# A recurrent-memory attention step on one core: output-projection weights cut by 4 heads x 512 outputs, and the chunks of two steps interleaved

## Chip, cores and metric

One core of a Trainium2 chip runs one program, one launch. The metric is device time in microseconds (us); the kernel before has a median of 2463.49 us in three runs (2462.24 to 2467.92).

## What is computed

```python
# x 2048 x 1024; 32 heads of 128; memory of M = 8 rows; segments of 32 rows; F = 3584
mem = mem0
for s in range(64):
    h = concat([mem, x[32*s : 32*s+32]])            # 40 rows
    q, k, v = h @ Wq, h @ Wk, h @ Wv                # 1024 -> 32 heads x 128
    p = softmax(mask(q @ k.T * 128**-0.5))          # per head, 40 x 40
    o = (p @ v) @ Wo                                # 4096 -> 1024
    mem = o[:8]; a[32*s : 32*s+32] = o[8:]
b = (gelu(x @ w_gate) * (x @ w_up)) @ w_down
g = sigmoid((x * gate_w).sum(-1))
out = g * a + (1 - g) * b
```

The 64 segments are serial: the first 8 rows of one segment's output are the memory rows of the next. The feed-forward part (`b`) is not.

## The kernel before, in words

A prologue turns and stores x, then 64 **steps** (one per segment) run, then the output projection of rows that were left out of the steps, then the feed-forward part with the final mix.

**Rows.** A step works on 32 columns: 24 rows of x and the 8 memory rows, in `hT` (8 chunks of 128 x 32). The other 8 rows of x of each segment need no memory; their k, q and v are computed for four segments at once by **fills** (`fill`, L689), and stored to DRAM (`qk_scr`, `v_scr`) to be read back by the steps (`load_qk`, `load_v`). The table `FILL` gives the steps two, two, one and one fill in turn, of eight matmul groups each; the two kinds of step are called two-fill and one-fill below. No fill is made in the last steps.

**Pieces.** The four weight matrices take 64 **pieces** of 128 x 2048 bf16 (512 KB); memory holds 50. So each matrix is cut in two halves of 16 heads (`u` = 0, 1) and eight pieces each (`i`), and some pieces of the two halves share a slot (`PAIRS`: 3 of k, 3 of q, 4 of v, 4 of o). A step does one half in round `r` = 0 and the other in `r` = 1; in the next step the halves change places. A shared slot's piece is used in `r` = 1 and again in the next step's `r` = 0, and then, through `spent`, SP fetches the other half's piece into the slot (`fetch`, L351), due in `r` = 1 of the same step. Per step that is 14 fetches of 512 KB. `seq` puts shared pieces first in `r` = 0 and last in `r` = 1.

**Order.** `ORDER` lists the groups of a step: k0 q0 v0 k1 q1 o0 v1 o1 (matrix and round), eight pieces each (L662 for k, q, v; L674 for o). All engines run their instructions in program order, with waits that a small planner (`_Prog`) derives from the memory regions that each operation reads and writes. Between pieces the lists `at` put the rest: ACT evacuates a finished group into `tok` (L561), PE transposes it (L578), DVE copies it to `kT` or `qT` (L564), GpSimd adds the rest columns (`put_rest`, L723); `scores` (L597, L602) then starts a chain on DVE and ACT (L606 to L622) that ends in `tA` and `tB`, and `attend` (L632, L637) multiplies by v and leaves `oT`. There are two such chains in a step, one per round.

**End of a step.** `o1` finishes one bank, ACT copies it to `a_bf`, PE transposes it (L837), DVE puts the 8 memory rows into `hT` (L840), and the next step's k0 begins. A part of the last fill's matmuls lies around these transposes; its result goes out of `oS` to DRAM in the next step (`pend`, `fill_evac`, `fill_put`, L700 and L719). `oS` and `vA` (v of round 0) are the same memory.

Of the kernel before, what the change touches and what calls it, by code (L numbers as in the profile page):

```python
# [195 lines left out]
def bass_gated_mix__memory_aug_recurrent_mem_tr__geglu_ffn__prompt_kernel(  # L196
# [34 lines left out]
    with ExitStack() as es:  # L231
# [16 lines left out]
        a_scr = nc.dram_tensor("a_scr", [NSEG, SEG, D], BF16)  # L248
# [21 lines left out]
        hT = al("hT", [128, KC, 32])  # L270
        hR = al("hR", [128, KC, 32])
        low = cur[0] = (cur[0] + 63) // 64 * 64
        qkr = al("qkr", [128, 2, 128])
        oRc = al("oRc", [128, NB, 32])
        vB = al("vB", [128, 2, 128])
        kT = al("kT", [128, 4, 4, LQ])
        qT = al("qT", [128, 4, 4, LQ])
        oT = al("oT", [128, 4, 4, LQ])
        tok = al("tok", [128, 512])
        vA = al("vA", [128, 4, 128], at=oT.off)  # L280
        pA = al("pA", [128, 8, 32], at=kT.off)
        pB = al("pB", [128, 288], at=kT.off + 512)
        E8 = al("E8", [128, 8, LQ], at=qT.off + 640)
        tA = al("tA", [128, 8, 32], at=qT.off)
        tB = al("tB", [128, 8, 32], at=qT.off + 512)
        a_bf = al("a_bf", [128, 256], at=qT.off)
# [8 lines left out]
        PAIRS = {"k": (1, 3, 5), "q": (0, 2, 5), "v": (0, 2, 4, 6), "o": (0, 2, 4, 6)}  # L295
# [5 lines left out]
        ORDER = (("k", 0), ("q", 0), ("v", 0), ("k", 1), ("q", 1), ("o", 0), ("v", 1), ("o", 1))  # L301
        walk = [(m, r, i) for m, r in ORDER for i in seq(m, r)]

        def at_step(p, s):
            m, r, i = walk[p]
            return (m, r ^ (s % 2), i)
# [13 lines left out]
        for s_ in range(NSEG):  # L320
            for p in range(64):
                k = at_step(p, s_)
                uses[home[k]].append(k)
# [6 lines left out]
        def src(k):  # L330
            m, u, i = k
            if m == "o":
                h0 = 16 * u + 2 * i
                return A_Wo[h0:h0 + 2].rearrange("h p f -> p h f")
            W = {"q": A_Wq, "k": A_Wk, "v": A_Wv}[m]
            return W[i * 128:(i + 1) * 128, 16 * u:16 * u + 16, :].rearrange("d h e -> d (h e)")

        def dst(t, k):
            return t[:, :].rearrange("p (h f) -> p h f", h=2) if k[0] == "o" else t[:, :]
# [4 lines left out]
        def fetch(n):  # L344
            k, t = uses[n][done[n]], slots[n]
            if paired(k):
                lane = f"sl{n}"
            else:
                lane = f"res{nlane[0] % 8}"
                nlane[0] += 1  # L350
            op("sp", lambda e: e.dma_start(dst(t, k), src(k)), wr=[t.r()], lane=lane)  # L351
# [80 lines left out]
        def load_h(s, eng="sp"):  # L432
            op(eng, lambda e: e.dma_start(hT[:, :, :].rearrange("p k c -> p (k c)"), xq_scr[s // 4, :, s % 4, :]),
               rd=[("D", "xq", s // 4)], wr=[hT.r()], lane=f"h{eng}")
# [5 lines left out]
        def load_qk(s, r, eng="pool"):  # L440
            u = r ^ (s % 2)
            op(eng, lambda e: e.dma_start(qkr[:, :, :], qk_scr[:, s, 2 * u:2 * u + 2, :]),
               rd=[("D", "qk", s // 4, 2 * u), ("D", "qk", s // 4, 2 * u + 1)], wr=[qkr.r()], lane=f"qkr{eng}")
# [11 lines left out]
        load_x(2)  # L455
        for n, p in enumerate(range(16)):
            first(at_step(p, 0))
            if n + 3 < NPX:
                load_x(n + 3)
        op("pe", tr_mem, rd=[pm.r(), ident.r()], wr=[BK(5)])  # L460
        op("dve", lambda e: e.tensor_copy(memT[:, :], PBV[5][:, 0:64]), rd=[BK(5)], wr=[memT.r()])
        for T in range(NT):
            do_x(T)
            load_x(T + NPX)
            if T == 0:
                load_h(0, "pool")
                op("dve", lambda e: e.tensor_copy(hT[:, :, NR:32], memT[:, :].rearrange("p (k c) -> p k c", k=KC)),
                   rd=[memT.r()], wr=[hT.r()])
        for p in range(16, 24):
            first(at_step(p, 0))  # L470
# [65 lines left out]
        def load_a(T):  # L536
            t = asb[T % 4]
            op("act", lambda e: e.dma_start(t[:, :], a_scr[4 * T:4 * T + 4].rearrange("s t f -> (s t) f")),
               rd=[("D", "a", s) for s in range(4 * T, 4 * T + 4)] + [("D", "ar", T // 4, h) for h in range(2)], wr=[t.r()],
               lane=f"al{T % 4}")  # L540
# [6 lines left out]
        rbs = [al(f"rb{i}", [128, D], at=kT.off + 2048 * i) for i in range(2)]  # L547
# [5 lines left out]
        def load_xo():  # L553
            for k in lost:
                op("sp", lambda e, k=k: e.dma_start(dst(xo[k], k), src(k)), wr=[xo[k].r()], lane=f"xo{k[2]}")
# [19 lines left out]
        def trans(to, how):  # L575
            def f(e):
                for j in range(4):
                    ins = e.transpose(PBV[TT][:, j * 128:(j + 1) * 128], tok[:, j * 128:(j + 1) * 128], ident[:, :])  # L578
                return ins
            op("pe", f, rd=[tok.r(), ident.r()], wr=[BK(TT)])  # L580
            i_ap = PBV[TT][:, 0:512].rearrange("p (j g c) -> p (j g) c", g=4, c=32)
            o_ap = to[:, :, :, 0:32].rearrange("p j g c -> p (j g) c")
            n = 4 * LQ
            if how == "both":
                act_copy(o_ap[:, 0:8], i_ap[:, 0:8], [BK(TT)], [to.r(0, 2 * n)])
                dve_copy(o_ap[:, 8:16], i_ap[:, 8:16], [BK(TT)], [to.r(2 * n, 4 * n)])
            else:
                cp[how](o_ap, i_ap, [BK(TT)], [to.r()])
# [5 lines left out]
        def scores():  # L594

            def f(e):
                e.matmul(PB[SS][:, 0:320].rearrange("p (a c) -> p a c", a=4), lhsT=ident[:, :],  # L597
                         rhs=mS[:, :].unsqueeze(1).to_broadcast([128, 4, 80]), start=True, stop=False, skip_group_check=True)
                for lo, hi, c in ((0, 32, 0), (32, 40, 40)):
                    for j in range(4):  # L600
                        for g in range(4):
                            ins = e.matmul(PB[SS][32 * g:32 * g + hi - lo, j * 80 + c:j * 80 + c + LQ], lhsT=qT[:, j, g, lo:hi],  # L602
                                           rhs=kT[:, j, g, :], start=False, stop=True, skip_group_check=True)
                return ins
            op("pe", f, rd=[qT.r(), kT.r(), ident.r(), mS.r()], wr=[BK(SS)])
            op("pool", lambda e: e.memset(pB[:, :].bitcast(FP32), 0.0), wr=[pB.r()])  # L606
# [6 lines left out]
            op("dve", lambda e: e.tensor_tensor(out=pA[:, :, :], in0=E8[:, :, 0:32], in1=b8(sm, 32), op=ALU.mult),  # L613
               rd=[E8.r(), st8.r(8, 16)], wr=[pA.r()])
            fin = op("dve", lambda e: e.tensor_tensor(
                out=pB[:, :].rearrange("p (j a) -> p j a", j=4)[:, :, 0:64].rearrange("p j (c k) -> p j c k", c=2)[:, :, :, 0:8],
                in0=E8[:, :, 32:40].rearrange("p (j c) k -> p j c k", c=2),
                in1=sm.rearrange("p (j c) -> p j c", c=2).unsqueeze(3).to_broadcast([128, 4, 2, 8]), op=ALU.mult),
               rd=[E8.r(), st8.r(8, 16)], wr=[pB.r()])
            op("dve", lambda e: e.transpose(tA[:, :, :].rearrange("p a c -> p (a c)"), pA[:, :, :].rearrange("p a c -> p (a c)")),  # L620
               rd=[pA.r()], wr=[tA.r()])
            op("dve", lambda e: e.transpose(tB[:, :, :].rearrange("p a c -> p (a c)"), pB[:, 0:256]),  # L622
               rd=[pB.r()], wr=[tB.r()], after=[fin])

        def attend(u):
            bo = (B0, B1, B2, SS)

            def f(e):
                for j in range(4):
                    for g in range(4):  # L630
                        r = slice(32 * g, 32 * g + 32)
                        e.matmul(PB[bo[g]][:, j * LQ:(j + 1) * LQ], lhsT=vA[r, j, :],  # L632
                                 rhs=tA[r, 2 * j:2 * j + 2, :].rearrange("p a c -> p (a c)")[:, 0:LQ],
                                 start=(j == 0), stop=False, skip_group_check=True)
                for g in range(4):
                    r = slice(32 * g, 32 * g + 32)
                    ins = e.matmul(PB[bo[g]][:, 0:4 * LQ].rearrange("p (j c) -> p j c", j=4)[:, :, 24:40], lhsT=vB[r, u, :],  # L637
                                   rhs=tB[r, :, :].rearrange("p (j a) c -> p j (a c)", a=2)[:, :, 24:40],
                                   start=False, stop=True, skip_group_check=True)
                return ins  # L640
            op("pe", f, rd=[vA.r(), tA.r(), tB.r(), vB.r()], wr=[BK(b) for b in bo])
# [7 lines left out]

        KQV = [x for x in ORDER if x[0] != "o"]  # L650
        bank_of = {}

        def proj(p, s):
            k = at_step(p, s)
            w = slots[home[k]]
            i = k[2]
            if k[0] != "o":
                h, bk = hT, bank_of[walk[p][:2]]

                def f(e):  # L660
                    for g in range(4):
                        ins = e.matmul(PB[bk][32 * g:32 * g + 32, :], lhsT=h[:, i, :], rhs=w[:, g * 512:(g + 1) * 512],  # L662
                                       start=(p % 8 == 0), stop=(p % 8 == 7))
                    return ins
                op("pe", f, rd=[h.r(), w.r()], wr=[BK(bk)])
            else:
                r = walk[p][1]
                gp_, jj = i // 2, i % 2

                def f(e):  # L670
                    for hh in range(2):
                        for g in range(4):
                            c = hh * 1024 + g * 256
                            ins = e.matmul(PB[XO][32 * g:32 * g + 32, 0:256], lhsT=oT[:, gp_, 2 * jj + hh, 0:32],  # L674
                                           rhs=w[:, c:c + 256], start=(r == 0 and p % 8 == 0 and hh == 0), stop=(r == 1 and p % 8 == 7 and hh == 1))
                    return ins
                n = 4 * LQ
                op("pe", f, rd=[oT.r(gp_ * n, (gp_ + 1) * n), w.r()], wr=[BK(XO)])
            spent(k)

# [14 lines left out]
        def fill_evac(m, u, G, b, st):  # L695
# [7 lines left out]
            else:  # L703
                act_copy(tok[:, :], PB[b][:, :], [BK(b)], [tok.r()])

        def fill_put(m, u, G, st):
# [3 lines left out]

            def f(e):
                for j in range(4):
                    ins = e.transpose(PBV[TT][:, j * 128:(j + 1) * 128], tok[:, j * 128:(j + 1) * 128], ident[:, :])
                return ins
            op("pe", f, rd=[tok.r(), ident.r()], wr=[BK(TT)])
            op("dve", lambda e: e.tensor_copy(st[:, :].rearrange("p (i x c) -> p x i c", i=4, x=16),
                                              PBV[TT][:, 0:512].rearrange("p (x i c) -> p x i c", x=16, i=4)), rd=[BK(TT)], wr=[st.r()])
            m4 = 2 * u + (0 if m == "q" else 1)
            op("pool", lambda e: e.dma_start(qk_scr[:, 4 * G:4 * G + 4, m4, :], st[:, :].rearrange("p (i y) -> p i y", i=4)),  # L719
               rd=[st.r()], wr=[("D", "qk", G, m4)], lane="fq")  # L720

        def put_rest(t, m):
            op("pool", lambda e: e.tensor_copy(t[:, :, :, 32:40].rearrange("p j g c -> p (j g) c"),  # L723
                                               qkr[:, m, :].rearrange("p (x c) -> p x c", c=8)),
               rd=[qkr.r()], wr=[t.r()])

        base_of = {mr: 8 * n_ for n_, mr in enumerate(ORDER)}
        pend = []
        FILL = ((("k", 1), ("q", 1)), (("q", 0), ("v", 0)), (("v", 1),), (("k", 0),))
        X, Y = A0, A1  # L730
        for s in range(NSEG):
            last = s == NSEG - 1
            at = {}
# [3 lines left out]
            bank_of.update({mr: (X, Y)[n % 2] for n, mr in enumerate(KQV)})  # L737
# [253 lines left out]
```

## Time and profile before

| | |
|---|---|
| median of three runs | 2463.49 us |
| profiled execution | 2468.72 us, of which the span of instructions is 2466.9 us |
| granted TensorE clock, mean | 0.975 |
| start of the first k0 that follows a memory update to that of the last (62 steps) | 139.5 to 1771.2 us, 26.3 us a step |
| in that stretch | PE busy 1379.0 of 1631.7 us, DMA share 0.85, 304 GB/s |
| from 1808 us on (feed-forward) | PE busy 636.3 of 658.0 us, DMA share 0.40 |
| PE busy over the span | 2100.7 us, 85% |

The profile gives one execution. PE is TensorE's matmuls, PEld its weight loads, SPq and POOLq the instructions by which SyncE and GpSimd issue DMAs. "L662" is a line of the kernel before. In a row of the timeline the columns are start, length, engine, line, operation, output and input, count, and in brackets the idle time of that engine before it with what ended it. In the windows view a row is a stretch of time with its length, the busy time of each engine, the granted TensorE clock, the share of the DMA engines and the GB/s.

### The profile page before, as it was taken

How to read it: one execution, taken by the hardware profiler on the slowest of the kernel's cores; microseconds unless marked ns; L12 is line 12 of the kernel's file. 1: busy time of each engine (PE TensorE's matmuls, PEld its weight loads, DVE VectorE, ACT ScalarE, POOL GpSimd, SP SyncE). 2: the span in 40 equal slices, each digit the busy share in tenths (PEclk: the TensorE clock that was granted, in tenths of full speed). 3: DMA queues.
4: the chain of work that ended last, by engine and by line, in shares of the span. 5: the costliest groups of instructions: out<-in, count | busy, mean ns of one | idle time of the engine just before them, and what ended most of it. 6: DMA issues, size and time to landing. Idle time of an engine off the chain costs nothing.

```text
span 2466.9 us, 76488 instructions
## 1 busy us (share of the span) xinstructions
PE 2100.7 (85%) x34796; PEld 1055.6 (43%) x34822; DVE 899.5 (36%) x2119; ACT 572.5 (23%) x1175; POOL 402.6 (16%) x822
## 2 busy tenths in 40 slices
PE   2588888888888888888888888888879999999998
PEld 1244444444444444444444444443454444444443
DVE  3233333333333333333333333333304436264462
ACT  1122222222222222222222222222203213032130
POOL 5222212212122122212222122221100000000000
PEclk9789999999999999999999999999989999999999
DMA  9878888888888888888888888988894260713506
GB/s 358 329 271 293 310 325 287 321 313 286 314 303 282 318 298 285 318 319 289 323 305 290 313 308 287 325 299 294 305 312 147 71 219 1 249 41 112 179 1 222
DMA packets 283524, 642.68 MB, mean 261 GB/s; under 512 B 26504, under 2 KB 80264, under 8 KB 283200
## 3 DMA queue, kind: packets, MB, share of 16 engines
q1 hardware_dynamic: 263008, 604.93, 68.3%
q0 software_dynamic: 9824, 17.97, 2.4%
q10 hardware_dynamic: 10368, 14.88, 1.7%
q8 instruction: 273, 4.47, 0.7%
q14 instruction: 51, 0.42, 0.0%
HBM read 606.29 MB, written 31.39 MB: 258 GB/s over the span
## 4 chain that ended last, share of the span: by engine, by line
PE 45%; DMA 41%; DVE 6%; issue 3%; ACT 3%; POOL 1%; SPq 0%; ACTq 0%; POOLq 0%
DMA sl<-in_A_Wq_dram 17%; DMA sl<-in_A_Wo_dram 15%; PE pb L908 13%; PE pb L662 8%; PE pb L674 7%; PE pb L945 7%; PE pb L689 4%; DMA qk_scr<-oS 3%; PE pb L867 2%; PE pb L578 2%; DMA v_scr<-oS 1%; DMA wd<-in_B_w_down_dram 1%; DMA xr_scr<-xr 1%; DMA sl<-in_A_Wk_dram 1%; ACT tok L561 1%
## 5 line engine op out<-in xcount | busy, mean ns | idle before, releaser
L662 PE MATMUL pb<-sl,hT 128*32 128x512 bf16 x12288 | 792.1, 385 | 77.2 <-DMA sl<-in_A_Wq_dram 32.7
L662 PEld LDWEIGHTS pb<-sl,hT 128*32 128x32 bf16 x12288 | 322.3, 97 | 393.5 <-DMA sl<-in_A_Wq_dram 47.8
L674 PE MATMUL pb<-sl,oT 128*32 128x256 bf16 x8192 | 297.1, 285 | 50.3 <-DMA sl<-in_A_Wo_dram 39.3
L561 ACT ACTIVATE tok<-pb 128x512 bf16<-128x512 f32 x320 | 191.3, 598 | 358.4 <-PE pb L662 304.5
L674 PEld LDWEIGHTS pb<-sl,oT 128*32 128x32 bf16 x8192 | 205.7, 100 | 126.3 <-DMA sl<-in_A_Wo_dram 61.0
L689 PE MATMUL pb<-sl,hR 128*32 128x512 bf16 x3072 | 227.4, 392 | 7.8 <-issue 4.0
L908 PE MATMUL pb<-xT,wg 128*128 128x512 bf16 x896 | 211.8, 379 | 8.4 <-DVE GT L924 8.4
L908 PE MATMUL pb<-xT,wu 128*128 128x512 bf16 x896 | 211.7, 379 | 0.0
L646 POOL COPY oRc<-oT 128x128 bf16<-128x128 bf16 x128 | 96.7, 756 | 623.6 <-DVE oT L564 623.6
L945 PE MATMUL pb<-wd,GT 128*128 128x512 bf16 x876 | 193.4, 379 | 5.7 <-DMA wd<-in_B_w_down_dram 4.6
L561 ACT ACTIVATE vA<-pb 128x512 bf16<-128x512 f32 x128 | 76.4, 597 | 285.5 <-DMA v_scr<-oS 104.2
L916 ACT ACTIVATE s<-pb 128x512 f32<-128x512 f32 x112 | 66.8, 596 | 319.9 <-PE pb L908 300.4
L564 DVE COPY qT<-pb 128x512 bf16<-128x512 bf16 x128 | 54.4, 425 | 235.2 <-PE pb L578 225.3
L908 PEld LDWEIGHTS pb<-xT,wg 128*128 128x128 bf16 x896 | 86.9, 98 | 116.4 <-DVE GT L924 12.8
L564 DVE COPY kT<-pb 128x512 bf16<-128x512 bf16 x128 | 54.4, 425 | 223.3 <-POOL kT L723 123.0
L945 PEld LDWEIGHTS pb<-wd,GT 128*128 128x128 bf16 x896 | 87.2, 98 | 111.9 <-DMA wd<-in_B_w_down_dram 8.3
L632 PE MATMUL pb<-tA,vA 32*128 32x40 bf16 x2048 | 36.0, 178 | 115.6 <-DVE tB L622 110.5
L908 PEld LDWEIGHTS pb<-xT,wu 128*128 128x128 bf16 x896 | 87.6, 98 | 105.7
L917 DVE SCALAR_TENSOR_TENSOR tp<-s,pb 128x512 f32<-128x512 f32 x112 | 77.0, 688 | 133.9 <-ACT s L916 133.8
L607 DVE TENSOR_REDUCE st<-pb 128x8 f32<-128x320 f32 x128 | 63.0, 492 | 164.3 <-PE pb L602 164.3
L609 ACT ACTIVATE E<-pb 128x320 bf16<-128x320 f32 x128 | 55.7, 435 | 241.9 <-DVE pb L608 241.8
L561 ACT ACTIVATE oT<-pb 128x160 bf16<-128x160 f32 x256 | 63.8, 301 | 193.2 <-PE pb L637 193.2
(77 smaller groups left out, 1761.8 us busy)
## 6 DMA issues: line engine op xcount, KB each, us to landing
sl<-in_A_Wv_dram SPq DMA_DIRECT2D x268, 512.0 KB, 11.0
sl<-in_A_Wo_dram SPq DMA_DIRECT2D x268, 512.0 KB, 7.2
sl<-in_A_Wk_dram SPq DMA_DIRECT2D x205, 512.0 KB, 5.7
sl<-in_A_Wq_dram SPq DMA_DIRECT2D x205, 512.0 KB, 8.9
wd<-in_B_w_down_dram SPq DMA_DIRECT2D x56, 1024.0 KB, 5.7
wg<-in_B_w_gate_dram SPq DMA_DIRECT2D x3, 1792.0 KB, 15.4
wu<-in_B_w_up_dram SPq DMA_DIRECT2D x3, 1792.0 KB, 14.2
qkr<-qk_scr POOLq DMA_DIRECT2D x65, 64.0 KB, 5.8
```

Of the source, the lines that this page charges most:

```text
L561: op("act", lambda e: e.activation(o, i, ACTF.Copy), rd=rd, wr=wr)
L564: op("dve", lambda e: e.tensor_copy(o, i), rd=rd, wr=wr)
L607: op("dve", lambda e: e.tensor_reduce(nm, sS, AX.X, ALU.max, negate=True), rd=[BK(SS)], wr=[st8.r(0, 8)])
L609: op("act", lambda e: e.activation(E8[:, :, :].rearrange("p a c -> p (a c)"), PB[SS][:, 0:320], ACTF.Exp, scale=scale), rd=[BK(SS)], wr=[E ...
L646: op("pool", lambda e: e.tensor_copy(oRc[:, :, 16 * u:16 * u + 16].rearrange("p c x -> p x c"), oT[:, :, :, 32:40].rearrange("p g j c -> p ...
L662: ins = e.matmul(PB[bk][32 * g:32 * g + 32, :], lhsT=h[:, i, :], rhs=w[:, g * 512:(g + 1) * 512], start=(p % 8 == 0), stop=(p % 8 == 7))
L674: ins = e.matmul(PB[XO][32 * g:32 * g + 32, 0:256], lhsT=oT[:, gp_, 2 * jj + hh, 0:32], rhs=w[:, c:c + 256], start=(r == 0 and p % 8 == 0 ...
L689: ins = e.matmul(PB[b][32 * g:32 * g + 32, :], lhsT=h[:, k[2], :], rhs=w[:, g * 512:(g + 1) * 512], start=(n == 0), stop=(n == 7))
L908: ins = e.matmul(PB[bk][:, 0:FB], lhsT=w[:, kc, cc:cc + 128], rhs=xT[:, :, :, kc, :].rearrange("p t i c -> p (t i) c"), start=(kc == 0), s ...
L916: op("act", lambda e, hg=hg: e.activation(s1[:, :], hg, ACTF.Square, scale=SQ), rd=[BK(bg)], wr=[s1.r()])
L917: op("dve", lambda e, hg=hg, t=t: e.scalar_tensor_tensor(out=t[:, :], in0=s1[:, :], scalar=1.0, in1=hg, op0=ALU.add, op1=ALU.mult), rd=[BK ...
L945: ins = e.matmul(PB[bank[2 * k + hf]][:, :], lhsT=GT[:, j, tb * 128:(tb + 1) * 128], rhs=w[:, jj, hf * 512:(hf + 1) * 512], start=(j == 0) ...
```

## The change

Wo's pieces hold 4 heads x 512 outputs where they held 2 heads x 1024. With that, the first four pieces of a half (`i` = 0..3) give outputs 0..511 and the last four outputs 512..1023. The shared slots become 2 of k, 2 of q, 6 of v and 4 of o (pieces 4..7); the sum stays 14. The groups of eight are cut in halves of four and are walked in the order `HEAD` + `BODY`: a step begins with the first half of k0, then does the second half of the **previous** step's o1, and then the first halves of q0 and v0, which need only chunks 0..3 of `hT`, before the second halves. So the memory rows come in two lots: `fold(s, 0)` and `next_mem(s, 0)` ahead of k0, `fold(s, 1)` and `next_mem(s, 1)` behind the o1 half. `hT` exists twice. A piece of Wo gives two partial sums on different partitions, which `fold` adds on DVE (two instructions of 64 x 256); ACT's copy to `a_bf` goes.

To make room, `tok` is gone: each evacuation goes to the memory of its target (`stage["k"]` is `kT`, `stage["q"]` is `qT`), `tA` and `tB` become one tile with one DVE transpose (`tAB`, in `qT`'s memory), the q columns of the rest are read from `qkr` directly, and GpSimd copies only k's. The last fill of a step now goes out through `qS`, not `oS`. All fills but the first of a two-fill step stand at the step's end. The shared Wo pieces are copied once to a DRAM scratch in steps 1 to 8 (`keep`) and from then on fetched from there in rows of 4 KB.

```diff
-        hT = al("hT", [128, KC, 32])
+        hT0 = al("hT0", [128, KC, 32])
+        vB = al("vB", [128, 2, 128])
+        hT1 = al("hT1", [128, KC, 32])
+        hT = (hT0, hT1)
+        part = tuple(al(f"part{n}", [128, 256], FP32, at=o) for n, o in enumerate((hT0.off, vB.off)))
...
-        tok = al("tok", [128, 512])
+        pAB = al("pAB", [128, 544], at=kT.off)
+        E8 = al("E8", [128, 8, LQ], at=qT.off + 384)
+        tAB = al("tAB", [128, 512], at=qT.off)
...
-        PAIRS = {"k": (1, 3, 5), "q": (0, 2, 5), "v": (0, 2, 4, 6), "o": (0, 2, 4, 6)}
+        PAIRS = {"k": (0, 1), "q": (0, 1), "v": (0, 1, 2, 3, 4, 5), "o": (4, 5, 6, 7)}
...
-        ORDER = (("k", 0), ("q", 0), ("v", 0), ("k", 1), ("q", 1), ("o", 0), ("v", 1), ("o", 1))
+        HEAD = [("k", 0, 0), ("o", 1, 1), ("q", 0, 0), ("v", 0, 0), ("k", 0, 1), ("q", 0, 1), ("v", 0, 1)]
+        BODY = [(m, r, h) for m, r in (("k", 1), ("q", 1), ("o", 0), ("v", 1)) for h in range(2)] + [("o", 1, 0)]
...
-                h0 = 16 * u + 2 * i
-                return A_Wo[h0:h0 + 2].rearrange("h p f -> p h f")
+                h0 = 16 * u + 4 * (i % 4)
+                return A_Wo[h0:h0 + 4, :, 512 * (i // 4):512 * (i // 4) + 512].rearrange("h p f -> p h f")
...
+        def load_piece(t, k, lane):
+            if k in kept:
+                op("sp", lambda e: e.dma_start(t[:, :], wo_scr[wo_at(k)]), rd=[("D", "wo", k)], wr=[t.r()], lane=lane)
+            else:
+                op("sp", lambda e: e.dma_start(dst(t, k), src(k)), wr=[t.r()], lane=lane)
+
+        def keep(k):
+            t = slots[home[k]]
+            op("sp", lambda e: e.dma_start(wo_scr[wo_at(k)], t[:, :]), rd=[t.r()], wr=[("D", "wo", k)], lane="wo")
+            kept.add(k)
...
+        def fold(s, b):
+            lo, hi = slice(64 * b, 64 * b + 64), slice(64 - 64 * b, 128 - 64 * b)
+            pt, cs = part[s % 2], slice(256 * b, 256 * b + 256)
+            op("dve", lambda e: e.tensor_copy(pt[lo, :], PB[XO][hi, cs]), rd=[BK(XO)], wr=[pt.r()])
+            op("dve", lambda e: e.tensor_tensor(out=a_bf[lo, :], in0=PB[XO][lo, cs], in1=pt[lo, :], op=ALU.add),
+               rd=[BK(XO), pt.r()], wr=[a_bf.r()])
+
+        def next_mem(s, b):
+            h = hT[(s + 1) % 2]
+            lo = slice(64 * b, 64 * b + 64)
+
+            def f(e):
+                for t in range(2):
+                    ins = e.transpose(PBV[TT][:, 64 * t:64 * t + 64], a_bf[lo, 128 * t:128 * t + 128], ident[lo, lo])
+                return ins
+            op("pe", f, rd=[a_bf.r(), ident.r()], wr=[BK(TT)])
...
+            on("q", 0, 4, lambda: evac(bank_of["k", 0], stage["k"], "act"))
+            on("v", 0, 4, lambda: trans(kT, "k"))
+            on("v", 0, 4, lambda: evac(bank_of["q", 0], stage["q"], "act"))
...
+            on("v", 0, 4, lambda: put_rest())
+            on("v", 0, 7, lambda: trans(qT, "q"))
...
+            on("k", 1, 0, lambda: evac(bank_of["v", 0], vA, "act"))
+            on("k", 1, 1, lambda: scores(ua))
...
+                on("v", 0, 5, lambda: load_qk(s, 1))
+            on("o", 0, 0, lambda: evac(bank_of["k", 1], stage["k"], "act"))
+            if s > 0:
+                on("o", 0, 0, lambda: attend(ua))
+            on("o", 0, 0, lambda: trans(kT, "k"))
+            on("o", 0, 0, lambda: put_rest())
+            on("o", 0, 0, lambda: evac(bank_of["q", 1], stage["q"], "act"))
+            on("o", 0, 3, lambda: trans(qT, "q"))
+            on("o", 0, 6, lambda: scores(ub))
+            on("v", 1, 0, some(f1, 3))
+            on("o", 1, 0, lambda: evac(bank_of["v", 1], vA, "act"))
+            on("o", 1, 0, some(f1, 3))
+            on("o", 1, 0, lambda: attend(ub))
+            on("o", 1, 0, some(f1, 8))
...
+            nx = dict(s=s + 1)
+            on("k", 0, 0, lambda: fold(s, 0), **nx)
+            on("k", 0, 0, some(f2, 4), **nx)
+            on("k", 0, 0, lambda: next_mem(s, 0), **nx)
+            on("k", 0, 0, some(f2, 4), **nx)
+            if fl:
+                on("k", 0, 0, lambda: fill_evac(*fl[-1], B0, "q"), **nx)
+                on("k", 0, 3, lambda: fill_put(*fl[-1], "q"), **nx)
+            on("q", 0, 0, lambda: fold(s, 1), **nx)
+            on("q", 0, 0, lambda: load_v(s + 1), **nx)
...
+            on("v", 0, 1, lambda: next_mem(s, 1), **nx)
```

`on(m, r, n, ...)` puts work ahead of piece `n` of a group (`n` from 4 is the second half); `f1` is the first fill of a two-fill step, `f2` the last fill of any step, and both are lists of matmul groups. Around the steps, `a_scr` is laid out by column groups, so that the final mix reads it with four DMAs of 64 KB for each block of 128 rows where it was one of 256 KB, and the rows left out are stored with four DMAs, not two, for each block.

## The prediction

> **What bounds the kernel now.** First the chain that ended last, from the page: its costliest links are two fetches.
>
> ```profile
> PE 45%; DMA 41%; DVE 6%; issue 3%; ACT 3%; POOL 1%; SPq 0%; ACTq 0%; POOLq 0%
> DMA sl<-in_A_Wq_dram 17%; DMA sl<-in_A_Wo_dram 15%; PE pb L908 13%; PE pb L662 8%; PE pb L674 7%; PE pb L945 7%; PE pb L689 4%; DMA qk_scr<-oS 3%; PE pb L867 2%; PE pb L578 2%; DMA v_scr<-oS 1%; DMA wd<-in_B_w_down_dram 1%; DMA xr_scr<-xr 1%; DMA sl<-in_A_Wk_dram 1%; ACT tok L561 1%
> ```
>
> Then the windows of one us, to see whether the DMA engines are full (last two columns: share, GB/s):
>
> ```profile
> 1308.00:1309.00 1.00, 0.22 (x20) 0.20 (x20) 0.72 (x3) 0.00 (x0) 0.00 (x0) 1.00 1.09 434
> ...
> 1321.00:1322.00 1.00, 0.47 (x16) 0.35 (x20) 0.00 (x0) 0.01 (x1) 0.73 (x1) 1.00 0.12 28
> ...
> 1323.00:1324.00 1.00, 1.00 (x21) 0.49 (x24) 0.19 (x1) 0.00 (x0) 0.00 (x0) 1.00 0.10 25
> ```
>
> They are full for about 20 us and nearly idle for some 5 us around the end of a step: fetches come late for their order, not too many for the bandwidth (14 x 0.524 MB at about 0.4 MB/us are 18 us of 26.3). Then PE's timeline of a two-fill step:
>
> ```profile
> 1297.24 0.60 PE L662 MATMUL pb<-sl,hT 128*32 128x512 bf16 x8
> ...
> 1304.19 0.31 PE L597 MATMUL pb<-mS,ident 128*128 128x320 bf16 x1
> ...
> 1308.78 0.27 PE L632 MATMUL pb<-tA,vA 32*128 32x40 bf16 x16 [1.10 <-DVE tB L622]
> ...
> 1310.95 0.40 PE L662 MATMUL pb<-sl,hT 128*32 128x512 bf16 x4 [0.87 <-DMA sl<-in_A_Wq_dram]
> ...
> 1313.47 0.31 PE L597 MATMUL pb<-mS,ident 128*128 128x320 bf16 x1
> ...
> 1317.88 0.28 PE L632 MATMUL pb<-tA,vA 32*128 32x40 bf16 x16 [0.73 <-DVE tB L622]
> ...
> 1321.53 0.40 PE L674 MATMUL pb<-sl,oT 128*32 128x256 bf16 x8 [0.76 <-DMA sl<-in_A_Wo_dram]
> ...
> 1323.82 2.98 PE L662 MATMUL pb<-sl,hT 128*32 128x512 bf16 x52
> ```
>
> The step takes 26.58 us: scores at 6.95, attend at 11.54, second scores at 16.23, second attend at 20.64, next k0 at 26.58. From scores to attend are 4.4 to 4.6 us of DVE and ACT that PE can't shorten. Read the same way, steps average 26.7 us (two-fill) and 25.9 (one-fill). The fourth view is ACT's timeline and the waits:
>
> ```profile
> 1305.77 0.60 ACT L561 ACTIVATE vA<-pb 128x512 bf16<-128x512 f32 x1 [3.03 <-DMA qk_scr<-oS]
> ...
> 1333.00 0.60 ACT L561 ACTIVATE vA<-pb 128x512 bf16<-128x512 f32 x1 [4.46 <-DMA v_scr<-oS]
> ```
> ```profile
> ACT vA L561 <- DMA v_scr<-oS: 104.2, 27, 6.2
> ...
> ACT vA L561 <- DMA qk_scr<-oS: 90.2, 28, 5.0
> ```
>
> In 55 steps the evacuation of v waits until the last fill's store has left `oS`, 8.53 us after k0 began here and 9.18 in the next step; over all steps with fills I read 8.7 for stores of k or q and 8.6 for v. It is mostly covered now, because `vA` is first needed at attend.
>
> **The change, part by part** (t = 0 at the start of k0).
>
> *Fetch waits go.* PE's waits on sl in the steps are 39.3 (Wo), 32.7 (Wq), 10.2 (Wk) and 8.4 us (Wv), 91 in all, and what hangs on them. Wo's four pieces are issued in o0 and are now due behind the next k0's first half, some 10 us later, where their landing takes 8.5 us in the chain. v's are due some 9 us after the last issue. No fetch wait is left; late next is the attention chain.
>
> *The end of a step.* Before: second attend to k0 5.9 us (two fills), 4.8 (one). After: attend to first Wo piece 0.74 (1318.62 - 17.88), four pieces 0.98, of which the last's result comes 0.46 after its start (1321.53 to ACT at 1321.99). `fold`: copy 0.40 and add 0.42, between the 160-element CAST's 0.32 and the 320-element TENSOR_TENSOR's 0.50, plus two hand-overs of 0.1; transposes 0.15 (L837's two took 0.29 at twice the columns); four fill groups 0.85, which hide `hT`'s copy (0.19). Sum 3.95; a two-fill step adds its first fill's transposes and wait, 0.75: 4.7. The second lot hides behind q0 and one v0 piece (1.07) up to some 0.2, which is inside the PE time below.
>
> *Between the attends.* Before 4.1 to 5.0 us from attend to second scores. After, `tok` is gone: ACT can evacuate k1 into `kS` only when the chain has read `pAB`, so attend is followed by 0.60 + 0.15 of ACT before the transposes; then ACT's two `oT` copies (0.50) and q1 into `qS` (0.60 + 0.15), transposes 0.33, three Wo pieces 0.73, and 0.3 for `oT` and hand-overs: 2.9, PE idle 0.5 of it. GpSimd's copies (0.76 + 0.30) fit beside it.
>
> *k0 to scores.* The new wait. q0 now goes into `qS` on ACT, and `qS` is where the last fill's store starts from (the order of ACT's instructions shows this wait on `fq` or on the four `fv` in each such step). Behind it on ACT stand v's evacuation and the exponential, and on PE the transposes of q: everything. PE alone would be there at 7.3 us (27 pieces of 0.213 to 0.245 are 5.9, transposes 0.8, short waits 0.6), 6.65 without a `fill_put`. So the step now turns on the landing L. From L: evacuation and hand-over 0.75, transposes to DVE 0.44, copy 0.42, hand-over 0.14: scores at L + 1.75.
>
> What is L after? It is 2.4 us from issue where the DMA engines are idle, 6.5 where they are full:
>
> ```profile
> qk_scr<-kS POOLq DMA_DIRECT2D x32, 128.0 KB, 2.4
> ...
> v_scr<-oS POOLq DMA_DIRECT2D x124, 32.0 KB, 5.5
> ...
> qk_scr<-oS POOLq DMA_DIRECT2D x30, 128.0 KB, 6.5
> ```
>
> Its issue doesn't move (2.03 us for q, k; from 1.11 for v). Ahead of it stood three k pieces; now two do, with q later. By the windows from 1297 on, 1.05 MB had been moved 4.9 us after k0 and 1.57 MB 6.3 after: one piece less is 1.4 us. The bounds are 0 (as now) and 4.1 (idle landing). I take the whole 1.4 for k and q (8.7 to 7.3), nearest to that row, and less than half, 0.6, for v (8.6 to 8.0), whose first store is issued before the third k piece anyway. The Trainium skill (DMA: Bandwidth & Descriptors, Queues, rings and completion order) speaks against this: engines round-robin between queue rows by packet, so what stands ahead on SP's row should not matter. The 4.1 us between the idle and the busy landing do not look like an even turn-taking, though no row here excludes it.
>
> *The step's sum*: L + 1.75 + 4.55 + 2.9 + 4.55 + end. Two-fill 7.3 + 13.75 + 4.7 = 25.75 (before 26.7), one-fill 8.0 + 13.75 + 3.95 = 25.7 (before 25.9). So about 29 x 0.95 + 30 x 0.2 = 34 us less.
>
> *The rest.* The last steps have no fill, hence no store to wait for: 4 x 1.5 = 6 us less. `keep` writes 0.5 MB in eight steps, 1.4 us of DMA each under 4 us of slack; Wo's rows are 1 KB until then: 8 x 0.5, bounds 0 and 1.4, +4. The second `qkr` load is now issued behind all ten k, q, v pieces; strictly behind them it would land at 16.7 and cost up to 0.6, after 5.8 us from issue (median of its row) nothing: I take 0, nearest to that row. The smaller final-mix DMAs lie under a PE that is 97% busy: 0 (-3 to 3).
>
> Sum -36, from the profiled 2468.7 to 2432.7; that run lies 5.2 above the median of those shown, so **2428 us**.
>
> **Rivals.** (1) *The store lands early.* If it is out by 6.4 us, PE is the limit up to scores and a step takes 24.2: 59 x 2.1 = 124 us less, 2338. For: it takes only 2.4 us on idle engines. Against: k's fetch still starts just ahead of it.
>
> (2) *Slower: the store lands as now.* Place: ACT's q0 evacuation. With L = 8.65 a two-fill step takes 27.1 and a one-fill step 26.35: +0.45 x 59 - 2 = +25 us, **2488**. It decides from L = 8.2 on, where the gain is gone. For: k's two pieces still fill the engines; 8.6 is what 55 waits show. By the Trainium skill's rule above (DMA: Bandwidth & Descriptors, Queues, rings and completion order) L stays, and this is the outcome.
>
> (3) *TensorE's clock.* Stretches at half clock follow windows of waiting (granted 0.50 in 1338 to 1341, after 1.5 us idle within 3). A one-fill step now waits 1.9 us in a piece before its second attend, 0.4 behind it: if 0.6 of those steps lose half of the next 2.4 us, 30 x 0.6 x 1.2 = +22, 2450. The Trainium skill (TensorE: Matmul & The Clock Gate, What's actually happening) asks a whole idle window of about 3.4 us; by that it doesn't come.
>
> (4) *It doesn't run ahead*: if `fold` takes twice as long, k0 waits 0.8 more in each step, 2478; the rows at both sides speak against it.
>
> **How the numbers follow.** Forecast (2405 to 2455) 0.40; store lands earlier (2338 to 2405) 0.25; rival 2 (2459 to 2495) 0.20; 3 and 4, or both with 2 (2445 to 2510) 0.15. Half a us in any step's term is 30 us, so the range reaches 2350 to 2490, leaving out about a tenth at each end. Within 0.2% (2458.6 to 2468.4) is what a measurement of this kernel can't tell from no change: 0.09 (0.03 of rival 2, 0.06 of 3 and 4). Faster: 0.40 + 0.25 + 0.03 of 3 and 4 = 0.68; slower: 0.17 + 0.06 = 0.23.
>
> **What would show it.** Right: no PE wait on sl in the steps; ACT's q evacuation waiting on the store at 7.3 to 8.0 us, scores at 9 to 9.8; attend to second scores 2.9; second attend to k0 4 to 4.7; steps near 25.7. Wrong: a landing under 6.5 or over 8.2, or a wait that I have at nothing (`qkr`, `fold`, Wo) ending a step.

## The result, and the profile after

The changed kernel takes **2532.3 us** (median of 4, 2520.4 to 2537.1) against 2463.2 for the kernel before: a ratio of 1.0269 [1.0229, 1.0310]. I had forecast 2428 in a range of 2350 to 2490. It is slower, and slower than any of my rivals had it.

Its profiled execution takes 2537.1 us, of which 2535.3 are the span; the mean granted TensorE clock is 0.947 (0.975 before). The stretch from the first k0 to the last has grown from 1631.7 to 1694.2 us, 27.3 a step where 26.3 were: 62 of the 68 us between the two spans. First the chain that ended last, to be held against the one shown of before:

```profile
PE 49%; DMA 22%; DVE 13%; ACT 7%; issue 5%; POOL 3%; ACTq 0%; SPq 0%; POOLq 0%; DVEq 0%
PE pb L931 13%; PE pb L691 8%; DMA v_scr<-qS 7%; PE pb L703 7%; DMA qk_scr<-qS 6%; PE pb L968 6%; PE pb L740 5%; DMA sl<-in_A_Wv_dram 4%; PE pb L612 3%; ACT qS L595 3%; DMA wd<-in_B_w_down_dram 2%; PE pb L891 2%; DVE tAB L653 2%; POOL v_scr L751 2%; PE pb L634 2%
```

The two fetches that led before (Wq 17%, Wo 15%) are gone; in their place stand the last fill's stores out of `qS`, 13% together. The waits of ACT and PE say the same (in total, how many, longest):

```profile
ACT qS L595 <- DMA v_scr<-qS: 107.7, 30, 4.9
...
ACT qS L595 <- DMA qk_scr<-qS: 59.6, 27, 5.7
```
```profile
PE pb L612 <- ACT qS L595: 133.1, 62, 5.2
...
PE pb L691 <- DMA sl<-in_A_Wv_dram: 7.0, 12, 1.5
...
PE pb L703 <- DMA sl<-wo_scr: 0.8, 1, 0.8
```

PE's 91 us of waiting for slots in the steps are down to 7.8. But the waits for the store, which had 4% of the chain in front of `vA` (55 of them), now stand in front of q's transposes (57), and PE waits 133 us there. One one-fill step in PE's timeline (start, duration; in brackets the idle time before and what ended it), with the store and ACT's evacuation behind it:

```profile
1479.57 1.23 PE L691 MATMUL pb<-sl,hT 128*32 128x512 bf16 x16
...
1490.70 0.40 PE L612 MATMUL pb<-ident,qS 128*128 128x128 bf16 x4 [4.22 <-ACT qS L595]
...
1492.01 0.45 PE L628 MATMUL pb<-mS,ident 128*128 128x320 bf16 x1
...
1496.84 0.27 PE L662 MATMUL pb<-tAB,vA 32*128 32x40 bf16 x16
...
1499.45 0.31 PE L628 MATMUL pb<-mS,ident 128*128 128x320 bf16 x1
...
1503.92 0.28 PE L662 MATMUL pb<-tAB,vA 32*128 32x40 bf16 x16 [1.65 <-DVE tAB L653]
...
1504.65 1.90 PE L703 MATMUL pb<-sl,oT 128*32 128x256 bf16 x32 [0.43 <-ACT oT L595]
1506.34 1.88 PE L740 MATMUL pb<-sl,hR 128*32 128x512 bf16 x16
...
1509.18 0.61 PE L691 MATMUL pb<-sl,hT 128*32 128x512 bf16 x8
```
```profile
1480.85 2.20 POOL L751 DMA_DIRECT2D v_scr<-qS  x4 [2.50 <-ACT qS L595]
```
```profile
1490.05 0.60 ACT L595 ACTIVATE qS<-pb 128x512 bf16<-128x512 f32 x1 [4.87 <-DMA v_scr<-qS]
```

k0 is at 1479.57, so GpSimd issues the four stores from 1.3 to 3.5 and q0 can be evacuated at L = 10.5 (8.0 forecast). Between the attends the step does what was foreseen (2.6 us from attend to second scores). At its end Wo's pieces and the fill take nearly twice their time: 1.90 and 1.88 us for work that takes 1.06 and 1.04 in an earlier one-fill step:

```profile
1396.03 1.06 PE L703 MATMUL pb<-sl,oT 128*32 128x256 bf16 x32 [0.43 <-ACT oT L595]
1396.92 1.04 PE L740 MATMUL pb<-sl,hR 128*32 128x512 bf16 x16
```

The windows at the ends of these two steps show why (PEclk, and DMA share and GB/s at the end of the line):

```profile
1503.90:1509.20 5.30, 4.86 (x90) 2.49 (x94) 1.57 (x5) 0.50 (x2) 0.76 (x1) 0.68 0.39 148
```
```profile
1397.00:1400.00 3.00, 2.88 (x58) 1.24 (x54) 1.02 (x3) 0.60 (x1) 0.06 (x1) 1.00 0.15 40
```

The clock is granted at 0.68 in the first and at 1.00 in the second. And the DMA engines are still little used at the end of a step: their share is 0.39 and 0.15 in these rows.

Over steps 2 to 58, the mean of each term of the prediction's sum (us), two-fill steps (they begin with a q or k store) and one-fill steps (they begin with v's):

| | L | L to scores | scores to attend | attend to second scores | to second attend | to next k0 | step |
|---|---|---|---|---|---|---|---|
| two-fill, forecast | 7.3 | 1.75 | 4.55 | 2.9 | 4.55 | 4.7 | 25.75 |
| two-fill, after | 7.94 | 1.62 | 4.64 | 2.85 | 5.10 | 4.84 | 26.99 |
| one-fill, forecast | 8.0 | 1.75 | 4.55 | 2.9 | 4.55 | 3.95 | 25.70 |
| one-fill, after | 9.05 | 1.91 | 4.99 | 2.73 | 4.53 | 4.64 | 27.85 |

### The profile page after: what moved, and what is told of

Its sections match the earlier page's. It is cut to its first block, busy times and chain, and to the rows that moved or that the text cites. A ratio compares the mean times of both kernels' runs of the same rounds, so it can differ in the third digit from the quotient of the medians.

```text
span 2535.3 us, 76865 instructions
## 1 busy us (share of the span) xinstructions
PE 2145.1 (85%) x34922; PEld 1083.0 (43%) x34948; DVE 1019.0 (40%) x2310; ACT 546.4 (22%) x1111; POOL 432.4 (17%) x821
## 4 chain that ended last, share of the span: by engine, by line
PE 49%; DMA 22%; DVE 13%; ACT 7%; issue 5%; POOL 3%; ACTq 0%; SPq 0%; POOLq 0%; DVEq 0%
PE pb L931 13%; PE pb L691 8%; DMA v_scr<-qS 7%; PE pb L703 7%; DMA qk_scr<-qS 6%; PE pb L968 6%; PE pb L740 5%; DMA sl<-in_A_Wv_dram 4%; PE pb L612 3%; ACT qS L595 3%; DMA wd<-in_B_w_down_dram 2%; PE pb L891 2%; DVE tAB L653 2%; POOL v_scr L751 2%; PE pb L634 2%
## 5 line engine op out<-in xcount | busy, mean ns | idle before, releaser
L691 PE MATMUL pb<-sl,hT 128*32 128x512 bf16 x12288 | 813.4, 401 | 19.5 <-issue 11.2
L691 PEld LDWEIGHTS pb<-sl,hT 128*32 128x32 bf16 x12288 | 338.7, 100 | 320.1 <-issue 77.4
L740 PE MATMUL pb<-sl,hR 128*32 128x512 bf16 x3072 | 235.2, 420 | 2.6 <-issue 2.2
L703 PEld LDWEIGHTS pb<-sl,oT 128*32 128x32 bf16 x8192 | 199.8, 98 | 73.9 <-ACT oT L595 35.5
L968 PE MATMUL pb<-wd,GT 128*128 128x512 bf16 x876 | 195.9, 381 | 11.6 <-DMA wd<-in_B_w_down_dram 10.5
L595 ACT ACTIVATE qS<-pb 128x512 bf16<-128x512 f32 x189 | 113.8, 602 | 396.1 <-PE pb L740 224.3
L595 ACT ACTIVATE kS<-pb 128x512 bf16<-128x512 f32 x161 | 96.1, 597 | 441.1 <-PE pb L691 294.3
L612 PE MATMUL pb<-ident,qS 128*128 128x128 bf16 x636 | 67.0, 231 | 135.3 <-ACT qS L595 133.1
L612 PEld LDWEIGHTS pb<-ident,qS 128*128 128x128 bf16 x636 | 38.0, 101 | 195.4 <-ACT qS L595 195.0
L714 DVE COPY part<-pb 64x256 f32<-64x256 f32 x128 | 54.0, 422 | 165.2 <-PE pb L703 161.7
```

The source lines that it names most:

```text
L595: op("act", lambda e: e.activation(o, i, ACTF.Copy), rd=rd, wr=wr)
L612: ins = e.transpose(PBV[TT][:, j * 128:(j + 1) * 128], st[:, j * 128:(j + 1) * 128], ident[:, :])
L703: ins = e.matmul(PB[XO][32 * g:32 * g + 32, 256 * b:256 * b + 256], lhsT=oT[:, j, x, 0:32], rhs=w[:, c:c + 256], start=(r == 0 and n == 0 ...
L740: ins = e.matmul(PB[b][32 * g:32 * g + 32, :], lhsT=h[:, k[2], :], rhs=w[:, g * 512:(g + 1) * 512], start=(n == 0), stop=(n == 7))
L968: ins = e.matmul(PB[bank[2 * k + hf]][:, :], lhsT=GT[:, j, tb * 128:(tb + 1) * 128], rhs=w[:, jj, hf * 512:(hf + 1) * 512], start=(j == 0) ...
```

## The experiments

The theories, by the letters that the expectations use: **A**, the store's wait in `qS` is the loss; **B**, the half clock that follows PE's waits is; **C**, the fetches don't get through; **D**, two limits lie behind one another, the store's wait at q0 and the landing of the fetched pieces (v's first), so that lifting one alone gains nothing; **E**, the store has nothing to do with it. All kernels start from the changed one; ratios are to the kernel before on the same chip. Terms are means as in the table above, over both kinds of step (2 to 58).

### A buffer for the store

A buffer of its own does not fit in the memory that is left, so one slot goes, and with it one more piece is fetched in each step. That alone first:

```diff
-"v": (0, 1, 2, 3, 4, 5)
+"v": (0, 1, 2, 3, 4, 5, 6)
```

> Control for the next run: one more piece of v shares a slot, so 15 fetches per step instead of 14, and 4 KB per partition come free; nothing else. Theory A (the changed kernel is slow because ACT's evacuation of q waits for the last fill's store to leave qS; PE idle there 133 us in 62 steps, 2.15 each) expects the same wait and the same time, 2532 us, 0 to +20 for the extra 0.5 MB per step. Theory B (the cost is TensorE's half clock: 272 us of half clock in the profiled run against 124 before) expects the same. Theory C (fetch bandwidth: the step has become bound by the DMA engines) expects 1.4 us more in each step, +85 us.

2555.5 us, 1.0353 [1.0318, 1.0387]. The fifteenth fetch alone costs some 21 to 23 us, a little more than A allowed and far from the 85 of C; second scores to second attend grow from 4.8 to 5.3. Then with the buffer:

```diff
+fS = al("fS", [128, 512]); stage["f"] = fS
-fill_evac(*fl[-1], B0, "q") ... fill_put(*fl[-1], "q")
+fill_evac(*fl[-1], B0, "f") ... fill_put(*fl[-1], "f")
```

> As the control, but the last fill of a step goes out through a buffer of its own (1 KB per partition), so that ACT's evacuation of q has no store to wait for. Theory A: no PE idle on qS over 0.3 us, scores at 7.6 to 8.2 us after k0 instead of 9.3 to 11.1, steps of 24.2 to 25.3 us instead of 27.3, 2340 to 2410 us in all. Theory B alone (the wait is covered later by the attention chain and only the clock costs): scores move but attend hardly does, gain below 50 us. Theory C: no gain over the control.

2553.4 us, 1.0340 [1.0319, 1.0362]: the same as the control. The store's wait is gone and scores come at 7.9 instead of 10.2, but second scores to second attend have grown from 5.3 to 7.25, which gives nearly all of it back. Chain and PE's waits:

```profile
DMA sl<-in_A_Wv_dram 30%; PE pb L693 15%; PE pb L933 13%; PE pb L970 6%; PE pb L705 6%; PE pb L742 6%; PE pb L614 3%; PE pb L893 2%; DMA wd<-in_B_w_down_dram 2%; ACT vA L597 1%; PE pb L726 1%; DMA xr_scr<-xr 1%; PE pb L664 1%; POOL gp L458 1%; ACT fS L597 1%
```
```profile
PE pb L693 <- DMA sl<-in_A_Wv_dram: 115.5, 139, 2.4
```

PE now waits 115.5 us for v's pieces. A alone does not hold: in this kernel, with seven of v's pieces shared, there is a second limit, which the store had hidden.

### The second limit

Two of v's fetches become two of Wo's, which is fetched with more lead (`keep` runs to step 12). First with the store still in `qS`, 14 fetches:

```diff
-"v": (0, 1, 2, 3, 4, 5), "o": (4, 5, 6, 7)
+"v": (0, 1, 2, 3), "o": (2, 3, 4, 5, 6, 7)
...
-if 1 <= s <= 8:
+if 1 <= s <= 12:
```

> From the changed kernel, still 14 fetches per step: two of them move from v (6 to 4 shared slots) to Wo (4 to 6, copied to the scratch in steps 1 to 12), so that 8 pieces instead of 10 are due by the end of v1. The store through qS stays. Theory D (two limits stand at one place: without the store's wait, the ten or eleven k, q, v pieces themselves land only at some 20 us, so removing one alone gains nothing) expects the store's wait to hold the step: 2505 to 2540 us, PE's 133 us on qS still there. Theory E (own buffer didn't help because of its fifteenth fetch, and the store is not the cause at all) expects a gain here of 2 x 1.4 us where v1 waits, which is only 7 us in all: also no change. So this run and the next go together.

2545.9 us, 1.0323 [1.0269, 1.0377]: nothing gained, L 8.7. Then with the buffer for the store too (v 0 to 4, 15 fetches):

> Both at once: the last fill goes out through its own buffer, and of the 15 fetches 2 are k's, 2 q's, 5 v's and 6 Wo's, so that 9 pieces are due by the end of v1. Theory D: scores at 7.9 us after k0, second scores to second attend back from 7.25 to 4.5 to 5.2 us, a step of 24.6 to 25.5 us instead of 27.4, 2370 to 2430 us in all. Theory E: no better than the own buffer alone, 2530 to 2555. A wait on Wo in o1 would show as PE waiting for wo_scr.

**2446.7 us, 0.9920 [0.9891, 0.9949]**. The four corners are 2532 (neither), 2553 (buffer), 2546 (fetches), 2447 (both): only both together gain, though this corner and the buffer's fetch one piece more than the other two. The cleaner pairs say the same: with the buffer, at 15 fetches, two pieces moved from v to Wo take the ratio from 1.0340 to 0.9920; with the store in `qS`, at 14, the same move gains nothing. Scores come at 8.4, second attend 5.1 after second scores, and the wait for v is down:

```profile
PE pb L693 <- DMA sl<-in_A_Wv_dram: 10.3, 14, 1.5
```

That is D. It also speaks against C: 683 MB move in this kernel and 647 in the changed one, so the engines could carry more; the pieces were late for their place.

### The store off the critical place

The fill of the one-fill steps is put around v1, into `kS`, and not at the step's end:

```diff
-f1 = fill(*fl[0][:2], A1) if two else []
-f2 = fill(*fl[-1][:2], B0) if fl else []
+f1 = fill(*fl[0][:2], A1) if fl else []
+f2 = fill(*fl[-1][:2], B0) if two else []
```

> From the changed kernel: in one-fill steps the fill takes the place of the first fill (its matmuls on both sides of v1, evacuated into kS at o1, stored while the DMA engines are nearly idle) and not the step's end. Theory A: in the steps that follow a one-fill step ACT waits for no store, scores come at 7.6 to 8.2 instead of about 10 us; the step's end is shorter by some 1 us in one-fill steps, second attend later by 0 to 0.8. Half of all steps gain 2 to 3 us: -60 to -90 us, 2440 to 2475. Theory B: the gain is as large only if the half-clock time falls with it, to 200 us or less; Theory C: no change.

2476.3 us, 1.0033 [1.0006, 1.0059], without any added memory: half of the waits are gone (69.2 us in 32, where 133.1 in 62 were), the step is back to 26.3. The second limit shows here too, with 14 fetches and in one kernel: in the steps relieved of the store L is 5.9 and second scores to second attend takes 6.0; in the others they are 8.5 and 4.85.

```profile
PE pb L612 <- ACT qS L595: 69.2, 32, 5.3
...
PE pb L691 <- DMA sl<-in_A_Wv_dram: 23.8, 28, 2.2
```

Both together, the buffer with the fetches of the 2446.7 us kernel and the early fill:

> As the run before, and the fill of one-fill steps stands around v1 (through kS) instead of at the step's end. Theory D: the end of a one-fill step (second attend to k0) falls from 5.3 to 3.6 to 4.2 us, its second chain grows to 5 at most: another 0 to 1 us in half of the steps, 2355 to 2430 us.

**2440.0 us, 0.9888 [0.9859, 0.9918]**: the fastest of all, 1.1% faster than the kernel before. Its interval overlaps with that of the 2446.7, so most of its gain is that of the buffer and the fetches.

Next, to clear the window in which the store has to land, the `hT` load and the `a_scr` store are moved from k0 and q0 to o1 and v1, on SP, on top of the early fill:

```diff
-on("k", 0, 4, lambda: load_h(s + 1))
+on("o", 1, 0, lambda: load_h(s + 1))
-on("q", 0, 0, lambda: op("pool", ... a_scr[s] ... a_bf ...))
+on("v", 1, 0, lambda: op("sp", ... a_scr[s - 1] ... a_bf ...))   # of the next step
```

> From the run with the early fill (2476): two small transfers leave the stretch in which k, q and v are fetched: the load of the next hT goes to o1, the store of a_bf to v1, both on SP. Theory D with small transfers slowing the fetches (0.28 MB per us while they run, 0.36 before the change): the store through qS lands 0.3 to 1 us earlier in the steps that still have it, and PE's 24 us on Wv go: 2440 to 2468 us. If the small transfers don't matter: 2470 to 2485.

2543.9 us, 1.0322 [1.0299, 1.0345]: worse by 68. Where a store is still waited for, L is no better (8.5 and 9.1, where 7.9 and 9.1 were), so those transfers did not hold it up. And the move made a wait of its own: `fold` may write `a_bf` only when its store has left, and that one, issued later and among SP's fetches, takes 8.1 us to land instead of 6.7. Chain and DVE's wait:

```profile
DMA a_scr<-a_bf 15%; PE pb L932 13%; PE pb L691 12%; PE pb L703 6%; PE pb L969 6%; DMA v_scr<-qS 4%; PE pb L612 3%; DMA qk_scr<-qS 3%; DMA wd<-in_B_w_down_dram 2%; PE pb L740 2%; PE pb L892 2%; DMA sl<-in_A_Wv_dram 2%; ACT kS L595 1%; DVE tAB L653 1%; ACT qS L595 1%
```
```profile
DVE a_bf L715 <- DMA a_scr<-a_bf: 54.6, 48, 4.1
```

### What sets L

Two kernels move only the issue of v's last-fill stores:

```diff
-op("pool", lambda e, g=g: e.dma_start(
+op("act" if st is stage["q"] else "pool", lambda e, g=g: e.dma_start(
```

> The changed kernel, with the last fill's four v stores issued by ACT and not by GpSimd, so that they stand on a queue without the vB load and the a_scr store. In the changed kernel GpSimd issues the four from 1.1 to 3.3 us after k0, and the step's q0 evacuation starts at 9.05 in these 30 steps, 5.7 after the last issue. Theory I (issue): the landing follows the last issue by a fixed time; ACT's rows show 0.36 to 0.5 us for one issue, so the last is out at 2.6 to 3.1 and q0 is evacuated at 8.3 to 8.8: 30 x 0.25 to 0.75, 2510 to 2525. Theory Q (queue): sharing GpSimd's queue with the two transfers behind it delays them: 1 us or more earlier, 2500 or less. Theory F (full engines): the landing is set by the fetches that fill the engines: no change, 2525 to 2540.

2609.2 us, 1.0590 [1.0564, 1.0615]. L in the steps that begin with v's store is 11.0, later by 2, though the last store is issued at 3.0 and not at 3.3. All three theories missed that. With `g > 1` in the condition, two on each queue:

> The changed kernel, with two of the last fill's four v stores on GpSimd and two on ACT, so that all four are issued in about 1.1 us, 1.1 us sooner than now. Theory I: q0's evacuation in the 30 steps that begin with a v store moves from 9.05 to about 8.0, what I had forecast for it; 30 x 1.05 = 32 less: 2500. Theory F: the landing stays near 9.05 and the time within 2525 to 2540. If the landing moves and the time doesn't, the second limit (v's pieces) takes it, as with the buffer of its own: scores at 9.8 and second scores to second attend longer than 4.55 by what was gained.

2503.7 us, 1.0144 [1.0106, 1.0182], as theory I had it, though the run before spoke against that theory: L of these steps falls from 9.05 to 8.12 and the time by 29. The timelines of ACT, a step with four on ACT and then one with two:

```profile
1334.42 2.10 ACTq L751 DMA_DIRECT2D v_scr<-qS  x4
...
1345.78 0.60 ACT L595 ACTIVATE qS<-pb 128x512 bf16<-128x512 f32 x1 [6.78 <-DMA v_scr<-qS]
```
```profile
1354.63 0.82 ACTq L751 DMA_DIRECT2D v_scr<-qS  x2
...
1361.18 0.60 ACT L595 ACTIVATE qS<-pb 128x512 bf16<-128x512 f32 x1 [1.98 <-DMA v_scr<-qS]
```

From the end of the issue to the evacuation are 9.3 us with four and 5.7 with two. The DMA records of the trace show a difference that goes with it. On ACT's queue a store goes out in packets of 256 bytes, 512 for the four; in the first two us in which they move, 75 to 81 of them start per us beside 60 to 78 of the fetches' 4096-byte packets; in the third it is two for one, and then it falls, to 52 beside 63 in the fifth and 20 beside 85 in the seventh; the mean over the 7 us (3.2 to 10.2) is 73 per us. Half as many take half as long (3.2 to 6.7 to 7.2). On GpSimd's queue the four are only 64 packets of 2048 bytes, which start from 4.4 to some 8 us: the issue lasts till 3.3, and a packet starts 3 to 5 us after its issue. Why so long after, no run settles. What is shown is that with an unchanged order on SP's queue the landing moves with the store's own issue and its own packets.

### The clock

Six groups of four matmuls, whose result is not read, ahead of q's transposes, where PE waits for the store:

```diff
+if s > 0:
+    on("v", 0, 7, lambda: warm(s, 6))
 on("v", 0, 7, lambda: trans(qT, "q"))
```

> From the changed kernel: six groups of matmuls whose result nobody reads (1.3 us of PE) stand ahead of the transposes of q, where PE is idle 2.15 us on average. The wait itself stays. Theory B (the clock): the half-clock time falls from 272 us to about 150, and the chain from scores to attend from 4.8 to 4.55, 0.5 to 0.9 us per step, -30 to -55 us. Theory A (the wait): the landing of the store sets scores whatever PE does, 2520 to 2545 us, and a few us more where the store had landed early.

2527.8 us, 1.0228 [1.0202, 1.0255], no difference that the intervals tell from the changed kernel. Half clock falls from 272 to 162 us and scores to attend from 4.82 to 4.47, its undisturbed length; L grows by 0.14. But the long ends stay: in 16 of 29 one-fill steps second attend to k0 takes 5.2 to 5.5 us, in the others 3.8 to 4.3, and here it is 17 of 29. So the dummies go in front of the second attend of those steps:

```diff
+if fl and not two:
+    on("o", 1, 0, lambda: warm(s, 6, A1))
 on("o", 1, 0, lambda: attend(ub))
```

> The changed kernel, with six groups of four matmuls (their result is not read) ahead of the second attend of the 29 one-fill steps, where PE waits 1.65 us. In the changed kernel the second attend to the next k0 is either 3.8 or 5.2 us in these steps, 16 of 29 the longer; one of the longer stretches (1503.9 to 1509.2) had a granted clock of 0.68. Theory B (the clock, after the wait): all ends become 3.8, 16 x 1.4 = 22 less: 2510. Rival: the long ends have another cause, or the dummies hold up attend: 2525 to 2545.

2518.0 us, 1.0193 [1.0161, 1.0226]: about 14 to 19 less, near the 22 of theory B, but only in part where B has it. In the changed kernel a half-clock stretch of 3.4 us lies in each of the 16 long ends and in none of the other 13; now none lies in any, which is what B says. Yet the ends still take 4.41 on average where they took 4.64, a gain of only 7 us: PE now waits 11.4 us there in 17 gaps for which the profile names no cause. The rest of the difference lies in the two-fill steps, which have no dummies (26.1 us, in the changed kernel 27.0), while one-fill steps are no shorter (28.1, there 27.85). These are two single executions, the slowest of its kernel's four and the fastest, so a part of the agreement with B may be luck.

Both, with two of v's stores on ACT:

> The two v stores on GpSimd and two on ACT (2503.7 alone), the dummies ahead of q's transposes and those ahead of the second attend, all together. If the mis-sized terms simply add: the ends give 22, first scores to attend 57 x (4.68 - 4.40) = 16 less: 2466, that is no change against the kernel before. If what comes earlier is taken by the wait for v's pieces: second scores to second attend grow beyond 4.9 and the time stays at 2490 to 2504.

2504.2 us, 1.0129 [1.0086, 1.0173]: no less than the stores alone. Ends are at 3.97 and half clock at 100 us, but L is 8.36 in one-fill steps and second scores to second attend 5.0: what the clock gave is taken by the store and v's pieces, as its rival said. In one-fill steps second scores to second attend takes 5.04 where it was 4.65 with the stores alone, and PE's waits there for v's pieces are 13.1 us where they were 8.7.

## Why the prediction was wrong

**The step that failed is "What is L after?"**: the term L was mis-sized, 7.3 and 8.0 forecast, 7.94 and 9.05 measured. I let the landing move with the pieces issued ahead of the store ("one piece less is 1.4 us"). For q and k it moved by half of that (8.7 to 7.94), for v not at all (8.6 to 9.05): there the time of the issue (2.2 us for four) and the store's own packets weigh, as the two runs that move the issue show, and the change touches neither. Why v's came 0.45 later than before stays open. Nor did the rate behind the 1.4 us hold: from 3 to 6 us after k0 SP's queue moved 338 to 352 KB per us on average in the kernel before and 256 to 303 in the changed one. By 29 x 0.64 + 30 x 1.05 the term L is 50 of the 104 us that were missed. The sentence of the Trainium skill that I had set aside (DMA: Bandwidth & Descriptors, Queues, rings and completion order: an engine takes its queue rows in turn, by packet) agrees with the first two us on ACT's queue, about one for one; the third, two for one, and the tail it does not give.

**Rival 2 named the outcome.** Its place (ACT's q0 evacuation), its mechanism and its point of decision (L = 8.2) were right; at 8.5 on average the store decides. That its one L of 8.65 is near this mean is partly luck: the two kinds of store moved apart, to 7.94 and 9.05. Its price of +25 was too low, for it left the other terms as forecast.

**Rival 3 came with it**, at the price I gave it: 16 of 29 one-fill ends at 5.2 instead of 3.8 are 22 us, and each of the 16 holds a half-clock stretch. Scores to attend in one-fill steps (4.99, undisturbed 4.38) lost another 17 by the same clock, which I had not priced: the long wait for the store makes half clock too. Half clock falls into that term in 25 of the 29 steps, and the other four take 4.38. I had treated the two as alternatives, yet the first brings the second. They do not add up to what removing both gains, as the last kernel shows.

**"No fetch wait is left"** was right for the changed kernel (7.8 us) and misleading: the wait was hidden, not gone. Had L come out early (rival 1), v's pieces would have taken it, as they did with the buffer (where one piece more is fetched). PE's own work up to scores was also taken too short: with the buffer scores come at 8.1 (with a `fill_put`) and 7.6 us, not at 7.3 and 6.65. Second scores to second attend in two-fill steps, 5.10 against 4.55, are 16 us. The clock has no part in that: no half-clock stretch falls there in any of the 28 steps. PE waits 4.1 us for v's pieces, in seven of the steps, and 13.3 us, in ten others, for nothing that the profile names ("issue"), as here:

```profile
1335.85 0.61 PE L703 MATMUL pb<-sl,oT 128*32 128x256 bf16 x13 [1.98 <-issue]
```

This wait stands in the middle of a piece's matmuls; the last section says what it goes with. All other such steps take 4.47.

**"Mostly covered now"** was too kind to the store in the kernel before. ACT's exponential stands behind `vA`'s evacuation, and scores to first attend took 4.9 (two-fill) and 5.4 us (one-fill) there on average, where the step shown has 4.59 and the least is 4.31.

**Right**: the fetch waits of before; L to scores (1.6 to 1.9; forecast 1.75); attend to second scores (2.79; forecast 2.9); the end of a two-fill step (4.84; 4.7), that of a one-fill step at full clock (3.8; 3.95); `fold`, `keep` and `qkr` don't end a step. The last step and the final mix took 11 us more than before in the profiled execution, where I had nothing; 6 of them are waits for `wd`, and their cause stays open.

## What to carry to other kernels

A store that frees a buffer is a wait like any other: ask what the next writer of that buffer blocks. Here the same landing had 4% of the chain in front of `vA`, and 13% and 133 us of PE in front of q's transposes. When a wait is taken away, look for the one that it covered, and test the two together: each alone gained nothing here, both gained 0.8%. And time a store's landing by its own issue and its own number of packets before you count what is queued elsewhere.

## What the runs showed of the hardware

- The same four stores are 64 packets of 2048 bytes on GpSimd's queue and 512 of 256 bytes on ACT's. On ACT's queue beside full fetches 75 to 81 start per us at first, about one for each packet of the fetches, and 73 on average. Four stores there landed 2 us later than on GpSimd's queue, and two on each landed 0.9 earlier.
- On GpSimd one of these stores takes 0.55 us to issue, four 2.2.
- Half clock comes in stretches of 3.4 us or multiples. In the 3.4 us ahead of 55 such stretches of the changed kernel's steps, PE was busy for 4 to 55%, median 39%. The stretches at full clock between them are whole multiples of 3.41 us too; cut into such windows, the 376 that no half clock followed have PE busy for 45% or more. The Trainium skill (TensorE: Matmul & The Clock Gate, What's actually happening) speaks of an idle window; here one that is less than about half busy was enough.
- PE's waits without a named cause go with the queue that the profile calls "instruction" (q8). In the steps of the changed kernel there are 25, 21.5 us in all, and each ends 2.2 to 2.7 us after a packet of 16 KB starts on that queue; of PE's 250 other waits 13 end 2.15 to 2.8 us after one. I take them for waits for PE's own instructions, which no run tests. They are 19.3 us (23) in the kernel before and 62.2 us (63) in the one of 2446.7 us, where they are far more than the wait for v's pieces.
